# Scores ahead of values in a decode attention loop, and the last projection ahead of the first piece of w4

## The chip, the cores and the metric

The kernel runs on one core of a Trainium2 chip; the other cores are idle. The metric is device microseconds of one execution. Every run quoted here was labelled "fast" (the undisturbed state). A clock of 0.50 means that the throttle granted TensorE half its clock in that stretch. A kernel's time is the median of its runs; a ratio of two kernels is the mean time of one kernel's fast runs over the mean of the other's fast runs of the same rounds, so it is not quite the ratio of the medians that are quoted. A profile's span is about 1.8 us shorter than the time of the same execution (209.6 us for 211.45 us), because it runs from the first to the last instruction.

## The reference, cut to what matters

Two branches read the same layer-normalised input and are added: a decode step of attention with a long K/V window, and an MLP mixer with one token.

```python
# x: (4, 1, 576).  A_k_cache, A_v_cache: (4, 16, 8192, 128) bf16, the last W = 2048 keys are used
xn = layernorm(x)
# A: 32 query heads, 16 K/V heads, head size 128
q = xn @ wq
p = softmax(q @ k[:, :, -W:].T * Dh**-0.5)
attn = (p @ v[:, :, -W:]) @ wo                  # wo: 4096 x 576
# B (one token, so the shifted groups are all zero and x1 = xn)
mlp = xn + gelu(layernorm(xn) @ w3) @ w4         # w3: 576 x 4608, w4: 4608 x 576
out = x + attn + mlp
```

All of it is done for four tokens. Arithmetic is small against the data: 16 K tiles and 16 V tiles of 2.1 MB each (2048 KB, called 2 MB below), wq 4.7 MB, wo 4.7 MB, w3 5.3 MB and w4 5.3 MB are read once, 87.17 MB in all.

## The kernel before: the parts that matter

One queue issues all large loads, in a fixed order. K and V tiles rotate through six buffers; a load waits until the buffer's last reader is done. w4 comes last, in six pieces, the last ones small, so that little work is left when the last byte arrives.

```python
NKV = 6
kvp = ctx.enter_context(tc.tile_pool(name="kv", bufs=NKV))
...
W4_PIECES = [0, NFH, NF - 12, NF - 6, NF - 2, NF - 1, NF]      # NFH = 18, NF = 36
order = [("K", 0), ("K", 1), ("K", 2)]
for h in range(Hkv):                                           # Hkv = 16
    order.append(("V", h))
    if h + 3 < Hkv:
        order.append(("K", h + 3))
```

The loop over K/V heads is a software pipeline. Step `t` turns K of head `t` (VectorE), makes its scores (TensorE), does the softmax of head `t-1`, the values of head `t-2` and the output of heads before. A step has four slices `s`. An engine takes its instructions in the order in which they stand here.

```python
for t in range(Hkv):
    hm, hv, hf, hp = t - 1, t - 2, t - 3, t - 4
    for s in range(NSL):
        ...                          # softmax of hm, o_scale(hf), K transposes on VectorE
        if hv >= 0:
            pv(hv, s)                # 4 matmuls, 32 x 512 out, reads V of head hv
        k_scores(t, s)               # 4 matmuls, 128 x 512 out, reads the transposed K of head t
        ...
    flush_loads()
```

After the loop, the softmax and the values of the last two heads are finished, `o_spread` and `o_pick` prepare the last attention output, and the output matmuls are added up in two PSUM tiles, `acc` and `acc_odd`, in pairs that run side by side in different columns of the array.

```python
o_spread(hl)                 # TensorE: R
o_pick(hl)                   # VectorE: two instructions, op <- R
mlp_out(*pieces[0])          # 36 matmuls with w4 rows 0..17
o_proj(hl)                   # 16 matmuls with the last wo tile; needs op
mlp_out(*pieces[1])          # 12
mlp_out(*pieces[2])          # 12
mlp_out(*pieces[3])          # 8
...                          # odd <- acc_odd
for lo, hi in pieces[4:]:
    mlp_out(lo, hi)          # 2 + 2, on acc alone
...                          # fin = acc + odd, store
```

## Time and profile before

| | before |
|---|---|
| time | 211.55 us, median of 3 (211.48 to 211.74) |
| profile span | 209.6 us |
| DMA: load queue, share of 16 engines' span | 97.6% |
| bytes loaded | 87.17 MB |
| TensorE busy | 145.8 us (70%) |
| VectorE busy | 113.6 us (54%) |

Lines of the page of before. The rows with digits cut the span into 40 slices, in tenths: busy share for an engine, granted clock for PEclk. The q1 line is the load queue: packets, MB, and the time of its packets as a share of 16 engines' span.

```profile
PE   0367297659691009659899898597883976979884
PEclk9999589996997556958999999799998596969999
DMA  7999999999999999999999999999999999999992
q1 hardware_dynamic: 6640, 87.17, 97.6%
```

The DMA row is full from the second slice to the last but one. TensorE, at 70%, has holes, and its granted clock falls to half now and then. The Trainium skill, "HBM Reference", section "Specifications (TRN2)", says that a core streaming alone measures about 425 GB/s. Here, counted from the first packet at 1.78 us, the stream moves 87.17 MB in 204.8 us, 426 GB/s. The stream runs at the rate that the page gives.

The issues of w4's six pieces in before (durations in ns, starts in us), with the time from issue to landing:

```profile
L141 SPq DMA_DIRECT2D w_sb<-in_B_w_dram x6: 327/376/587, 170.7 to 184.5; - x6
...
DMA to landing us min/median/max: 22.0/30.3/32.6
```

The last piece, issued at 184.5, landed 22.0 us later, at 206.5. What follows it is short and fixed. The chain of waits of before (start, length, what) blames TensorE's output matmuls for the end:

```profile
205.51 0.12 PE acc L183
...
205.88 0.28 PE acc L183
```

But the timeline of before (start, length, engine, line, instruction) has a step of 0.29 us between 205.59 and 205.88, where all other pairs follow each other after 0.12 us:

```profile
205.46 0.29 PE L183 MATMUL acc<-w_sb,gT 128*8 128x288 bf16 x1
...
205.59 0.29 PE L183 MATMUL acc<-w_sb,gT 128*8 128x288 bf16 x1
...
205.88 0.28 PE L183 MATMUL acc<-w_sb,gT 128*8 128x288 bf16 x1
...
207.08 0.43 DVE L617 TENSOR_TENSOR fin<-acc,odd 8x288 bf16<-8x288 f32 x1
207.55 0.36 SPq L618 DMA_DIRECT2D out_dram<-fin  x1
```

The matmul at 205.88 is the first of w4's fourth piece, which landed at 205.84. TensorE has caught up with the loads by then, and the loads set the end.

Two of before's waits (us in total, times, longest) say what TensorE waits for in the loop: V tiles, not K. In these names vn is a V tile and kn a K tile as loaded, kt a K tile turned, S scores and O values.

```profile
PE O L394 <- DMA vn<-in_A_v_cache_dram: 36.2, 10, 15.4
PE S L342 <- DVE kt L226: 4.8, 3, 4.2
```

### The profile page before, as it was taken

To read this page: it belongs to the slowest core of one execution; us is meant where nothing else is said; L and a number is where in the kernel's file an instruction comes from. 1 tells how busy PE (TensorE), PEld (TensorE's weight loads), DVE (VectorE), ACT (ScalarE), POOL (GpSimd) and SP (SyncE) were. 2 spreads that over 40 slices of the span, in tenths; PEclk is the share of its full clock that TensorE was granted. 3 is DMA by queue.
4 is the path that set the end of the run, shared out by engine and by line. 5 is a ranking of instruction groups with operands and counts; after the bars stand their busy time and mean duration, and the time that the engine had idled before them with its cause. 6 is when DMAs were issued, how large, how long until landed. Compare 5 with 4: busy or idle time off the path is not lost.

```text
span 209.6 us, 2332 instructions
## 1 busy us (share of the span) xinstructions
PE 145.8 (70%) x941; PEld 62.6 (30%) x955; DVE 113.6 (54%) x165; ACT 34.4 (16%) x66; POOL 8.9 (4%) x33
## 2 busy tenths in 40 slices
PE   0367297659691009659899898597883976979884
PEld 0122132223240003214364233143431321425363
DVE  4501877892840082834903898658579174671420
ACT  7702201010220000202102222020211020202310
POOL 5600000000000000000000300000000000000000
PEclk9999589996997556958999999799998596969999
DMA  7999999999999999999999999999999999999992
GB/s 301 400 428 422 444 422 419 435 438 420 471 401 421 437 425 422 441 438 425 435 425 431 431 417 436 435 435 427 422 447 422 417 440 441 419 435 449 410 402 76
DMA packets 6658, 87.31 MB, mean 417 GB/s; under 512 B 748, under 2 KB 1016, under 8 KB 1656
## 3 DMA queue, kind: packets, MB, share of 16 engines
q1 hardware_dynamic: 6640, 87.17, 97.6%
q8 instruction: 7, 0.11, 0.2%
q14 instruction: 3, 0.02, 0.0%
q10 hardware_dynamic: 8, 0.00, 0.0%
HBM read 87.17 MB, written 0.00 MB: 416 GB/s over the span
## 4 chain that ended last, share of the span: by engine, by line
DMA 60%; PE 26%; DVE 9%; ACT 2%; issue 1%; SPq 0%; DVEq 0%; ACTq 0%
DMA vn<-in_A_v_cache_dram 38%; DMA w_sb<-in_B_w_dram 16%; PE S L342 9%; DMA wq_sb<-in_A_wq_dram 6%; PE acc L183 5%; DVE kt L226 5%; PE O L394 3%; PE g_ps L460 2%; PE q_ps L286 2%; PE oT L407 2%; DVE mx L348 1%; DVE PT L376 1%; PE S L364 1%; DVE qz L318 1%; PE gT_ps L472 1%
## 5 line engine op out<-in xcount | busy, mean ns | idle before, releaser
L342 PE MATMUL S<-kt,qz 128*128 128x512 bf16 x242 | 75.4, 435 | 7.2 <-DVE kt L226 4.8
L226 DVE STREAM_TRANSPOSE kt<-kn 128x2048 int32<-128x2048 int32 x32 | 73.0, 2285 | 13.5 <-DMA kn<-in_A_k_cache_dram 12.1
L394 PE MATMUL O<-vn,PT 128*32 128x512 bf16 x256 | 27.2, 425 | 38.8 <-DMA vn<-in_A_v_cache_dram 36.2
L342 PEld LDWEIGHTS <-qz 128*128 128x128 bf16 x256 | 21.9, 104 | 44.2 <-issue 28.1
L370 ACT ACTIVATE E<-S 128x512 bf16<-128x512 f32 x16 | 9.5, 597 | 120.9 <-PE S L364 120.9
L394 PEld LDWEIGHTS <-PT 128*32 128x32 bf16 x256 | 7.3, 95 | 48.2 <-issue 41.0
L376 DVE STREAM_TRANSPOSE PT<-E 128x512 bf16<-128x512 bf16 x16 | 11.4, 710 | 15.9 <-ACT E L370 15.9
L417 DVE TENSOR_REDUCE on<-oT 128x8 bf16<-128x128 f32 x16 | 4.6, 289 | 22.0 <-PE oT L407 22.0
L401 ACT ACTIVATE O_sb<-O,rd 128x512 f32<-128x512 f32 x16 | 11.0, 686 | 15.7 <-PE O L394 15.7
L348 DVE TENSOR_REDUCE mx<-S 128x1 f32<-128x512 f32 x16 | 10.5, 658 | 1.4 <-PE S L342 1.4
L407 PE MATMUL oT<-ident_w,O_sb 128*128 128x128 f32 x64 | 10.8, 295 | 0.4 <-ACT O_sb L401 0.3
L407 PEld LDWEIGHTS oT<-ident_w,O_sb 128*128 128x128 f32 x64 | 8.7, 155 | 5.5 <-issue 2.7
L360 DVE TENSOR_REDUCE nm<-mg 8x1 bf16<-8x16 f32 x16 | 2.3, 141 | 11.4 <-PE mg L355 11.4
L364 PE MATMUL S<-nm,j_row 8*128 8x512 bf16 x16 | 6.1, 381 | 2.4 <-DVE nm L360 2.3
L183 PE MATMUL acc<-wo_sb,op 128*8 128x288 bf16 x56 | 7.5, 286 | 0.0
L380 PEld LDWEIGHTS dn<-rs,same_j 128*128 128x128 f32 x32 | 5.8, 189 | 2.9 <-ACT E L370 0.7
L330 PE MATMUL S<-negbig,ohT 4*128 4x512 bf16 x16 | 6.2, 385 | 0.2 <-issue 0.2
L286 PE MATMUL q_ps<-wq_sb,xnT 128*32 128x512 bf16 x40 | 4.2, 596 | 1.8 <-DMA wq_sb<-in_A_wq_dram 1.8
L183 PEld LDWEIGHTS <-op 128*8 128x8 bf16 x64 | 4.7, 87 | 2.2 <-issue 0.3
L183 PE MATMUL acc<-w_sb,gT 128*8 128x288 bf16 x38 | 5.1, 286 | 0.0
L478 DVE COPY g_x<-gT_ps 128x64 f32<-128x64 f32 (+1 forms) x3 | 0.6, 194 | 8.4 <-PE gT_ps L472 8.4
L460 PE MATMUL g_ps<-w_sb,ln2T 128*32 128x512 bf16 (+1 forms) x50 | 4.9, 445 | 0.0
(93 smaller groups left out, 81.9 us busy)
## 6 DMA issues: line engine op xcount, KB each, us to landing
kn<-in_A_k_cache_dram SPq DMA_DIRECT2D x16, 2048.0 KB, 22.8
vn<-in_A_v_cache_dram SPq DMA_DIRECT2D x16, 2048.0 KB, 24.8
wo_sb<-in_A_wo_dram SPq DMA_DIRECT2D x4, 1152.0 KB, 25.4
w_sb<-in_B_w_dram SPq DMA_DIRECT2D x1, 4608.0 KB, 33.4
wq_sb<-in_A_wq_dram SPq DMA_DIRECT2D x1, 4096.0 KB, 12.7
w_sb<-in_B_w_dram SPq DMA_DIRECT2D x1, 2592.0 KB, 29.6
w_sb<-in_B_w_dram SPq DMA_DIRECT2D x2, 864.0 KB, 31.8
w_sb<-in_B_w_dram SPq DMA_DIRECT2D x2, 576.0 KB, 32.6
```

The costliest lines, as they stand in the source:

```text
L183: nc.tensor.matmul(out=to[q:q + OR, :], lhsT=lhsT[:, NI - 1 - i:NI - 1 - i + OR], rhs=rhs[:, i * CW:(i + 1) * CW], start=start, stop=False ...
L226: nc.vector.transpose(out=kt[:], in_=src)
L286: nc.tensor.matmul(out=q_ps[r][g * QD:(g + 1) * QD, :], lhsT=xnT[:, k, :], rhs=wq_sb[:, col:col + NW], start=(j == 0), stop=False, skip_gr ...
L342: nc.tensor.matmul(out=S_ps[h][:], lhsT=qz[:, z0:z0 + P], rhs=kt[:, ib, c0:c0 + SC, e:2 * QD:2].rearrange("p c k -> p (c k)"), start=False ...
L348: nc.vector.reduce_max(out=mx[:], in_=S_ps[h][:], axis=AX.X)
L364: nc.tensor.matmul(out=S_ps[h][:], lhsT=j_row[:], rhs=st.pop(("nm", h))[:, 0:1].to_broadcast([NJ, NW]), start=False, stop=False, skip_grou ...
L370: nc.scalar.activation(out=E[h][:].rearrange("p c k -> p (c k)"), in_=S_ps.pop(h)[:], func=ACT.Exp, scale=scale, accum_out=rs[:])
L376: nc.vector.transpose(out=PT[h][:], in_=E.pop(h)[:])
L394: nc.tensor.matmul(out=O_ps[h][g * QD:(g + 1) * QD], lhsT=PT[h][:, c, :], rhs=vn[:, :, c, :], start=(s == 0), stop=False, skip_group_check ...
L401: nc.scalar.activation(out=O_sb[h][:], in_=O_ps.pop(h)[:], func=ACT.Copy, scale=st.pop(("rd", h))[:, 0:1])
L407: nc.tensor.transpose(out=oT[:, s, :], in_=o[:, s, :], identity=ident_w[:, s * NJ:s * NJ + P])
L460: nc.tensor.matmul(out=g_ps[g * QD:(g + 1) * QD], lhsT=ln2T[:, k, :], rhs=rhs, start=(j == 0), stop=False, skip_group_check=True)
```

## The change

The intent: values need V of head `t-2`, whose load comes after that of K of head `t`. With the values first in each slice, TensorE can stand in front of a V tile with scores ready behind it. The change puts the scores of a slice first and does the values one slice later, the last two slices of values together. At the end, the last output projection, 16 matmuls whose weights came long ago, goes ahead of w4's first piece.

```diff
-            if hv >= 0:
-                pv(hv, s)
             k_scores(t, s)
+            if hv >= 0 and s > 0:
+                pv(hv, s - 1)
+                if s == NSL - 1:
+                    pv(hv, s)
...
     o_spread(hl)
     o_pick(hl)
+    o_proj(hl)
     mlp_out(*pieces[0])
-    o_proj(hl)
     mlp_out(*pieces[1])
```

No instruction is added or removed; only TensorE's order changes.

## The prediction

> **What bounds the kernel now.** The DMA stream. The page has the core's 16 DMA engines busy at 9 tenths or more in every one of the 40 slices but the first and the last, and the one big load queue takes 97.6% of 16 engines' span. It moves 87.17 MB; landing times of the loads (issue time plus time to landing, by tile) show 2 MB tiles landing every 4.85 us without a gap, and the last piece of w4, issued at 184.5, landing 22.0 us later, at 206.5. The Trainium skill, "DMA: Bandwidth & Descriptors", section "Measured", has 425 GB/s for one core's 16 MB load; here it is 87.17 MB over 204.8 us, 426 GB/s: no room is left in the stream. What follows the last landing is fixed: the last two output matmuls, VectorE's fin (207.08 to 207.52), the store's issue at 207.55, span end 209.6.
>
> The chain of waits puts the last 5 us down to "PE acc" (201.1 to 206.7), as if TensorE's output matmuls bound the end. The timeline says no: these start in pairs every 0.12 us, but between 205.59 and 205.88 there is a step of 0.29 us: a 0.17 us pause for the fourth piece of w4. TensorE has caught up with the DMA before the end.
>
> **What the change does.** No work is added or removed; TensorE's order alone changes.
> 1. In each loop step the scores of a slice no longer stand behind values that may not have landed. TensorE waits 36.2 us in total for V tiles (waits view); it can now do two slices of scores (8 matmuls, 2 to 3.8 us by clock) first. At the last step it stood until 184.53 for V13, though the transposed K was ready near 183.4. I estimate scores 15 done near 192 instead of 194.4, by removing this 1.1 us and by having one value slice (0.4 us) or more fewer ahead of each score slice.
> 2. V buffers are freed by the last values of a step, which now come after the last scores: 1.1 to 1.9 us later relative to these, partly made up by item 1. Loads wait from 17 to 41 us between issue and landing (by tile), against 4.85 us of own transfer, so at least some 12 us of queued work shield the stream. I expect no gap.
> 3. At the end, o_proj waits for o_pick. Before, VectorE's two o_pick instructions (201.16 to 202.04) hid behind the first piece of w4 (2.2 us of matmuls). Now TensorE idles some 0.95 us there, then runs o_proj (16 matmuls, 0.97 us), then the first piece. By itself that would make TensorE's end about 0.8 us later; item 1's lead of 2 us or so (less where V15, landing near 194.3, now gates) pays for it. The pieces behind it still land at about 202.3, 204.4, 205.8 and 206.5, and the last ones set the end.
>
> **On the critical path:** nearly nothing, at most 0.1 us gained; at worst, if item 1's lead isn't there, 0.8 us lost.
>
> **Predicted:** 211.5 us, range 211.1 to 211.9. Faster by over 2%: 0.01; within 2%: 0.98; slower by over 2%: 0.01.
>
> **What would show it.** Right: w4's last landing within 0.3 us of 206.5; TensorE's wait for V tiles much smaller; an idle of about 1 us before o_proj; scores 15 done 2 us earlier; a clear wait for DMA before the second to fourth piece of w4. Wrong: a hole in the DMA row, a last landing that moved, or output matmuls back to back up to fin.
>
> **What would make it wrong:** the queue running dry because V buffers free late; a lower granted clock around 190 to 200, putting o_proj's delay on the end; a different DMA rate.

## The result, and the profile after

| | before | after |
|---|---|---|
| time, median of 6 | 211.56 us (211.47 to 211.74) | 211.57 us (211.44 to 211.75) |
| ratio | | 1.000 (0.9987 to 1.0013) |
| profile span | 209.6 us | 209.9 us |
| first load lands | 3.97 us | 4.25 us |
| last load lands | 206.55 us | 206.81 us |
| between the two | 202.58 us | 202.55 us |
| scores of head 15 end | 194.41 us | 190.60 us |

Same time. The 0.3 us by which the profiled execution of after is longer is there when the first load lands, and stays.

The page of after, the lines that answer to those above. The DMA row is as full as before.

```profile
PE   0378198699670039649998999659995976898684
PEclk9999769999996557976999999999997968899969
DMA  8999999999999999999999999999999999999991
q1 hardware_dynamic: 6640, 87.17, 97.5%
```

w4's issues in after, and their time to landing:

```profile
L141 SPq DMA_DIRECT2D w_sb<-in_B_w_dram x6: 327/328/587, 168.5 to 184.6; - x6
...
DMA to landing us min/median/max: 22.2/31.7/34.6
```

w4's first piece was issued 2.3 us earlier than before (168.46 for 170.75), and only waited longer in the queue. The waits of after, of TensorE and of VectorE's K transposes:

```profile
PE S L342 <- DVE kt L226: 31.3, 13, 15.0
DVE kt L226 <- DMA kn<-in_A_k_cache_dram: 25.0, 8, 14.6
PE O L394 <- DMA vn<-in_A_v_cache_dram: 8.4, 8, 3.0
```

The wait for V fell from 36.2 to 8.4 us, and the wait for transposed K rose from 4.8 to 31.3 us; behind that one stands VectorE's own wait for K loads (12.1 us before). The idle time was moved from one kind of load to the other: these two waits of TensorE add up to 41.0 us before and 39.7 us after.

The end of after in the timeline (idle time before an instruction and what ended it are in brackets):

```profile
194.51 1.05 PE L394 MATMUL O<-vn,PT 128*32 128x512 bf16 x16 [0.62 <-DMA vn<-in_A_v_cache_dram]
...
198.76 0.29 PE L183 MATMUL acc<-wo_sb,op 128*8 128x288 bf16 x1 [0.97 <-DVE op L439]
...
200.70 0.40 PE L183 MATMUL acc<-w_sb,gT 128*8 128x288 bf16 x1 [0.78 <-DMA w_sb<-in_B_w_dram]
...
200.89 0.44 PE L183 MATMUL acc<-w_sb,gT 128*8 128x288 bf16 x1
201.13 0.44 PE L183 MATMUL acc<-w_sb,gT 128*8 128x288 bf16 x1
...
205.84 0.29 PE L183 MATMUL acc<-w_sb,gT 128*8 128x288 bf16 x1
...
206.12 0.28 PE L183 MATMUL acc<-w_sb,gT 128*8 128x288 bf16 x1
```

TensorE reaches the end 3.3 us earlier than before (the values of head 15 start at 194.51, before at 197.84). Then it waits for the last V tile, for `o_pick`, and for w4's first piece, which lands only at 200.65. After these waits the pairs of output matmuls follow each other after 0.24 us and not 0.12 us, until about 204. At 205.84 to 206.12 there is again a small pause for the fourth piece: it just fits.

Why 0.24 us? The windows view gives, for the stretch just before and the stretch itself, busy time and count of each engine, the granted clock (PEclk), the DMA share and GB/s. First before, then after:

```profile
198.00:200.70 2.70, 2.13 (x24) 1.12 (x17) 0.57 (x2) 0.81 (x2) 0.00 (x0) 1.00 0.94 397
200.70:204.00 3.30, 3.23 (x58) 2.42 (x59) 0.86 (x3) 0.00 (x0) 0.00 (x0) 1.00 0.99 405
```

```profile
198.00:200.70 2.70, 1.15 (x18) 0.73 (x18) 0.67 (x2) 0.00 (x0) 0.00 (x0) 0.98 0.89 370
200.70:204.00 3.30, 3.30 (x28) 1.90 (x29) 0.00 (x0) 0.00 (x0) 0.00 (x0) 0.50 1.00 419
```

In after TensorE was busy only 1.15 of the 2.70 us before w4's first piece, and then had half its clock for 3.4 us: 28 matmuls in a stretch in which before did 58. So the equal times needed an explanation after all. Was the loop's gain eaten by the end, or was nothing there to gain?

### The profile page after: what moved, and what is told of

The parts are those of the page before. It is cut to its first block, busy times and chain, and to the rows that moved or that the text cites. A ratio compares the mean times of both kernels' runs of the same rounds, so it can differ in the third digit from the quotient of the medians.

```text
span 209.9 us, 2326 instructions
## 1 busy us (share of the span) xinstructions
PE 149.1 (71%) x941; PEld 60.2 (29%) x955; DVE 113.7 (54%) x165; ACT 34.4 (16%) x66; POOL 8.9 (4%) x33
## 4 chain that ended last, share of the span: by engine, by line
DMA 52%; PE 24%; DVE 19%; issue 2%; ACT 1%; SPq 0%; DVEq 0%; ACTq 0%
DMA vn<-in_A_v_cache_dram 19%; DMA w_sb<-in_B_w_dram 15%; DVE kt L226 14%; DMA kn<-in_A_k_cache_dram 12%; PE S L342 9%; DMA wq_sb<-in_A_wq_dram 6%; PE acc L183 4%; PE O L394 2%; PE g_ps L460 2%; PE q_ps L286 2%; DVE mx L348 2%; PE S L364 1%; PE oT L407 1%; DVE PT L376 1%; DVE dm L350 1%
## 5 line engine op out<-in xcount | busy, mean ns | idle before, releaser
L342 PE MATMUL S<-kt,qz 128*128 128x512 bf16 x242 | 74.0, 429 | 34.5 <-DVE kt L226 31.3
L342 PEld LDWEIGHTS <-qz 128*128 128x128 bf16 x256 | 24.0, 108 | 63.5 <-issue 46.6
L394 PE MATMUL O<-vn,PT 128*32 128x512 bf16 x256 | 22.9, 400 | 8.4 <-DMA vn<-in_A_v_cache_dram 8.4
L394 PEld LDWEIGHTS <-PT 128*32 128x32 bf16 x256 | 5.9, 94 | 29.6 <-issue 28.6
L407 PEld LDWEIGHTS oT<-ident_w,O_sb 128*128 128x128 f32 x64 | 7.0, 146 | 4.6 <-issue 3.9
L183 PE MATMUL acc<-w_sb,gT 128*8 128x288 bf16 x38 | 6.6, 342 | 0.8 <-DMA w_sb<-in_B_w_dram 0.8
L380 PE MATMUL dn<-rs,same_j 128*128 128x1 f32 x32 | 6.4, 268 | 0.0
L380 PEld LDWEIGHTS dn<-rs,same_j 128*128 128x128 f32 x32 | 5.2, 204 | 4.1 <-issue 3.4
L183 PE MATMUL acc_odd<-w_sb,gT 128*8 128x288 bf16 x34 | 6.1, 350 | 0.0
```

Of the source, the lines that this page charges most:

```text
L183: nc.tensor.matmul(out=to[q:q + OR, :], lhsT=lhsT[:, NI - 1 - i:NI - 1 - i + OR], rhs=rhs[:, i * CW:(i + 1) * CW], start=start, stop=False ...
L342: nc.tensor.matmul(out=S_ps[h][:], lhsT=qz[:, z0:z0 + P], rhs=kt[:, ib, c0:c0 + SC, e:2 * QD:2].rearrange("p c k -> p (c k)"), start=False ...
L380: nc.tensor.matmul(out=dn[:], lhsT=same_j[:], rhs=st.pop(("rs", h))[:], start=True, stop=True)
L394: nc.tensor.matmul(out=O_ps[h][g * QD:(g + 1) * QD], lhsT=PT[h][:, c, :], rhs=vn[:, :, c, :], start=(s == 0), stop=False, skip_group_check ...
L407: nc.tensor.transpose(out=oT[:, s, :], in_=o[:, s, :], identity=ident_w[:, s * NJ:s * NJ + P])
```

## The experiments

Theory A, that of the prediction: the stream of loads sets the end, and TensorE's order is hidden behind it. Rival B: the loop's part gains time, and the swap at the end takes it back. Each kernel was timed beside runs of before on the same chip.

### One half of the change at a time

`loop_only` has the first hunk of the diff, `end_only` the second.

> The loop's new order without the swap at the end. Theory A (the load stream sets the end, TensorE's order is hidden behind it): same as before within 0.15 us, the last landing of w4 2.0 us or more after TensorE could have taken it, a wait of 2 us or more for w4's first piece. Theory B (the loop's part gains, the swap at the end takes it back): 0.5 to 1.5 us faster than before, about 210.5.

> The swap at the end without the loop's new order. Both theories: TensorE idles 0.95 us before o_proj and nothing pays for it; before had only a 0.17 us pause there, so the end should come 0.8 us later, 212.3 us, if the granted clock stays full; the last landing of w4 does not move. A third theory C (all that TensorE does at the end is hidden): 211.55.

| kernel | median us | lowest to highest | ratio to before |
|---|---|---|---|
| before (11 runs) | 211.63 | 211.43 to 212.00 | |
| loop_only (6) | 212.96 | 212.39 to 213.43 | 1.0064 (1.0049 to 1.0079) |
| end_only (6) | 212.02 | 211.49 to 214.11 | 1.0034 (1.0002 to 1.0067) |

Both were misses. The loop's half alone is slower, by 1.3 us, where A had the same time and B a gain. The swap is not what takes a gain back; it is what keeps the loop's half from costing. The stream hardly moved: in `loop_only` the last load landed at 207.02, 202.88 us after the first, which is 0.3 us more than in before. Most of the time is lost after TensorE's wait for w4's first piece. Timeline of `loop_only`:

```profile
197.67 0.35 PE L426 MATMUL R<-on,sel_wo 128*128 128x32 bf16 x8 [0.38 <-DVE on L417]
200.91 0.28 PE L183 MATMUL acc<-w_sb,gT 128*8 128x288 bf16 x1 [2.89 <-DMA w_sb<-in_B_w_dram]
...
201.40 0.45 PE L183 MATMUL acc<-w_sb,gT 128*8 128x288 bf16 x1
...
201.64 0.45 PE L183 MATMUL acc<-w_sb,gT 128*8 128x288 bf16 x1
```

and its windows, the same stretches:

```profile
198.00:200.70 2.70, 0.02 (x1) 0.03 (x1) 0.85 (x2) 0.00 (x0) 0.00 (x0) 1.00 0.90 372
200.70:204.00 3.30, 3.09 (x28) 1.93 (x29) 0.00 (x0) 0.00 (x0) 0.00 (x0) 0.56 1.01 424
```

TensorE came 3 us early, stood 2.89 us, and then had all 88 output matmuls in front of it with half its clock for 3.4 us: 14 pairs at 0.24 us, 14 x 0.12 = 1.7 us lost. With o_proj behind w4's first piece, the last matmul ended at 208.37, against 207.03 in before. Of these 1.34 us, 0.47 are the later last landing of this one execution, and 0.87 are work that was left after it (1.35 us from the last landing to the end of the matmuls, 0.48 in before). In after the 16 matmuls of o_proj ran inside the wait, so only 72 were left, and these just made it.

`end_only` has three runs at the time of before (211.49 to 211.62) and three above it (212.43, 212.74, 214.11). Its profile is of one of the slower ones (212.43), and shows a clock of 0.50 from 200.7 to 204.0 after the 0.97 us idle before o_proj:

```profile
198.00:200.70 2.70, 1.15 (x16) 0.84 (x18) 1.41 (x4) 0.14 (x1) 0.00 (x0) 1.00 0.94 395
200.70:204.00 3.30, 3.30 (x30) 1.82 (x28) 0.00 (x0) 0.00 (x0) 0.00 (x0) 0.50 0.99 410
```

The other five runs have no trace, so why three of them took no longer than before is not shown. Theory E: what loses time is the halved clock, falling on the output matmuls. Its rival F: the order of `loop_only` is too long for the time left after 200.9 at any clock.

### Keeping TensorE busy, or taking the wait away

`loop_fill` and `end_fill` are those kernels with filler matmuls into a scratch PSUM tile that nobody reads (12 and 4 of them); `after_fill` has 4 fillers before o_proj and 4 after it.

```diff
+    def keep_warm(n):
+        w = ps_m.tile([P, NW], F32, tag="m", name="warm")
+        for _ in range(n):
+            nc.tensor.matmul(out=w[:], lhsT=ident_bf[:], rhs=qz[:, 0:NW], start=True, stop=True)
...
     o_pick(hl)
+    keep_warm(12)                 # loop_fill
     mlp_out(*pieces[0])
```

`loop_split` removes the wait in another way: w4's first piece is loaded as three.

```diff
-    W4_PIECES = [0, NFH, NF - 12, NF - 6, NF - 2, NF - 1, NF]
+    W4_PIECES = [0, 6, 12, NFH, NF - 12, NF - 6, NF - 2, NF - 1, NF]
...
-    mlp_out(*pieces[0])
+    for i in range(3):
+        mlp_out(*pieces[i])
     o_proj(hl)
...
```

> loop_only with 12 matmuls of 512 columns into a scratch PSUM tile, read by nobody, put where TensorE idled 2.9 us before w4's first piece. Theory E (loop_only lost its 1.4 us because the granted clock was 0.5 for 3.41 us right after that idle, so that 14 pairs of output matmuls took 0.24 us each and not 0.12): no halved clock after 200, pairs at 0.12 us, 211.5 to 211.7. Rival F (the order first piece, then o_proj, is too long for the time left after 200.9 at any clock): 88 matmuls of 0.06 us are 5.4 us, so the end stays at about 213, or later by the filler's overrun.

> loop_only with w4's first piece of 18 rows loaded as three of 6, so that TensorE can begin on the first third at about 198. It takes away the wait, not the clock. Theories E and F both: 211.4 to 211.8, since 1.5 us of matmuls move ahead of 200.9. If it stays above 212.4, both are wrong and the loop's order costs something elsewhere.

> end_only with 4 such filler matmuls where TensorE idled 0.97 us before o_proj. end_only ran from 211.5 to 214.1. Theory E: that spread is the halved clock falling on the output matmuls or not; with the filler it narrows to 211.5 to 211.8. Rival: the spread has another cause and stays, over 1 us from lowest to highest.

> The changed kernel with 4 filler matmuls before o_proj and 4 between o_proj and w4's first piece. The changed kernel's profile has the halved clock from 200.6 to 204.0, yet it ended with the stream. Theory A: with a full clock TensorE waits clearly for w4's second, third and fourth piece, and the time is the same as before within 0.15 us. Rival G (the halved clock ate a gain that the change would have had): 210.5 to 211.

| kernel | median us | lowest to highest | ratio to before |
|---|---|---|---|
| before (11 runs) | 211.63 | 211.44 to 212.14 | |
| loop_fill (5) | 211.52 | 211.48 to 211.61 | 0.9991 (0.9978 to 1.0004) |
| loop_split (5) | 211.78 | 211.73 to 211.88 | 1.0003 (0.9991 to 1.0015) |
| end_fill (6) | 211.69 | 211.50 to 212.55 | 1.0007 (0.9990 to 1.0024) |
| after_fill (5) | 211.53 | 211.44 to 211.71 | 0.9992 (0.9980 to 1.0004) |

Twelve useless matmuls make `loop_only` 1.4 us faster (the two were timed on different chips, but before took 211.63 us in the median on both). Its windows and timeline with the filler:

```profile
198.00:200.70 2.70, 2.41 (x15) 1.05 (x14) 0.46 (x2) 0.00 (x0) 0.00 (x0) 1.00 0.91 375
200.70:204.00 3.30, 3.30 (x58) 2.56 (x54) 0.00 (x0) 0.00 (x0) 0.00 (x0) 1.00 1.01 421
```

```profile
197.42 2.75 PE L492 MATMUL warm<-qz,ident_bf 128*128 128x512 bf16 x12
200.47 0.28 PE L183 MATMUL acc<-w_sb,gT 128*8 128x288 bf16 x1 [0.29 <-DMA w_sb<-in_B_w_dram]
...
205.90 0.28 PE L183 MATMUL acc<-w_sb,gT 128*8 128x288 bf16 x1 [0.49 <-DMA w_sb<-in_B_w_dram]
```

The clock stays full, 58 matmuls fit into the stretch again, and TensorE waits 0.49 us for the fourth piece. E holds, and F falls: at a full clock, the order of `loop_only` is done in time. `loop_split` agrees: without the long wait the loop's half costs nothing either, and its profile has the full clock from 178.4 us to 209.

`after_fill` answers the question left by the profile of after. With a full clock from 178.6 to 209.3 us (its profile) it is no faster: rival G, that the halved clock ate a gain, falls. TensorE then starts w4's third and fourth piece late for no other reason than the loads: steps of 1.14 us at 203.44 and 0.76 us at 205.19, where pairs otherwise follow after 0.12 us.

```profile
204.58 0.28 PE L183 MATMUL acc<-w_sb,gT 128*8 128x288 bf16 x1 [0.85 <-DMA w_sb<-in_B_w_dram]
...
205.95 0.28 PE L183 MATMUL acc<-w_sb,gT 128*8 128x288 bf16 x1 [0.47 <-DMA w_sb<-in_B_w_dram]
```

`end_fill` is inconclusive. Its profiled run has the full clock, as E wants, and four of its six runs lie between 211.50 and 211.77; but two lie at 212.28 and 212.55, so the spread is still 1.05 us, just over the bound set for the rival. These two runs have no trace. In before's own profile a halved clock falls on the last loop step (0.50 from 184.9 to 188.3), a place that this filler does not reach; it may be that. It stays open.

What comes before a halved stretch? In each of the fourteen traces the halved stretches last 3.41 us or a whole multiple of it, and they lie on one grid of 3.41 us, whose place differs from trace to trace. So the window to look at is the step of that grid just before (from the clock records and the windows view; before_4buf and after_no_v15 are kernels of the next sections):

| trace | grid step, us | TensorE busy in it, of 3.41 us | clock of the next step |
|---|---|---|---|
| loop_only | 197.71 to 201.12 | 0.52 | 0.50 |
| after | 197.17 to 200.58 | 1.50 | 0.50 |
| end_only | 197.29 to 200.70 | 1.80 | 0.50 |
| after_no_v15 | 197.30 to 200.71 | 2.44 | 1.00 |
| loop_fill | 198.57 to 201.98 | 3.12 | 1.00 |
| before | 181.51 to 184.92 | 1.91 | 0.50 |
| loop_split | 202.25 to 205.66 | 1.92 | 1.00 |
| before_4buf | 196.34 to 199.75 | 2.52 | 0.50 |

The first five, all at the wait for o_pick or for w4's first piece, follow the busy time: after_no_v15 idled the same 0.97 us before o_proj and kept its clock. The last three show that it is no clean threshold. That the grid lies elsewhere in each execution may be why end_only and end_fill scatter; no run here tests it.

### A shorter stream: is there a lead on TensorE at all?

`before_no_v15` and `after_no_v15` do not load the last V tile; head 15 uses V of head 14. The result is wrong (the comparison with the reference is too loose to notice one head). That takes 2 MB or 4.85 us out of the stream.

```diff
-        order.append(("V", h))
+        if h < Hkv - 1:
+            order.append(("V", h))
...
         kv_tiles[kind, h] = t
+        if (kind, h) == ("V", Hkv - 2):
+            kv_tiles["V", Hkv - 1] = t
```

> Before, with the last V tile not loaded (head 15 uses V of head 14; wrong result on purpose): 2 MB or 4.85 us fewer in the stream. Theory A: the stream ends 4.85 us earlier but TensorE's chain, which began its output matmuls at 201.05, hardly moves: 211.0 to 211.5, only 0.1 to 0.6 us faster. Theory C: 206.7.

> The changed kernel with the same 2 MB taken away. Theory A: the change's lead on TensorE, hidden so far, comes out: 208 to 209 us, 2.5 to 3.5 us faster than the kernel before with the same cut. Theory D (the change gives TensorE no lead worth the name): the same as that kernel within 0.5 us.

In the profiles w4's last piece landed at 201.93 and 201.92 us, 4.6 and 4.9 us earlier than in before and after. before_no_v15 took 210.25 us in the median (210.14 to 211.92, 6 runs), after_no_v15 208.90 (208.83 to 208.96, 4 runs). The last output matmuls of before_no_v15, then of after_no_v15, end 5.1 and 2.1 us after that:

```profile
206.37 0.65 PE L185 MATMUL acc<-w_sb,gT 128*8 128x288 bf16 x4
```

```profile
203.41 0.65 PE L185 MATMUL acc<-w_sb,gT 128*8 128x288 bf16 x4
```

So with the loads out of the way TensorE's chain is the end in both, and the change is worth 1.35 us by the medians (1.6 us by the means, 210.51 and 208.90). Both misjudged in size: I had expected 2.5 to 3.5 us from the profile of before, and before_no_v15 at 211.0 or more. Its profiled run is the slowest of its six, 211.92 us, and has the halved clock of the last loop step (0.50 from 185.1 to 188.5) that before's profile has too; the other five took 210.14 to 210.29. It is likely that this one stretch overstated TensorE's backlog by about 1.7 us (3.41 us at half the clock loses 1.7), but the five others have no trace to show that they lack it. The lead is real and hidden: theory A, with theory D (no lead) fallen. Both hunks of the change are in it; their shares were not taken apart here.

### Fewer buffers: does the new order free V later?

The prediction's second item feared that V buffers free later. With fewer K/V buffers the queue of waiting loads is shorter, and the time of freeing begins to count. The edit is `NKV = 6` to 4, and to 3.

> Before with 4 K/V buffers for 6. Loads waited at least 17 us from issue to landing; two buffers fewer take 2 x 4.85 us of that, so the estimate is 2 to 3 us of queued work left at the worst place. Theory A: 211.5 to 213. If the stream runs dry: above 214.

> The changed kernel with 4 K/V buffers. Theory H (scores no longer wait behind values, so a step ends earlier and V buffers come free earlier on the clock, as issue times of the changed kernel's trace are 0.6 to 2.2 us earlier from 113 to 158 us): the same as or up to 2 us faster than before_4buf. Theory I (my prediction's item 2: freed later): 0.5 to 2 us slower than before_4buf.

> Before with 3 K/V buffers: no queue left, the stream has holes and a step's order on TensorE is on the path. 225 to 260 us, an estimate with little behind it; DMA row with holes.

> The changed kernel with 3 K/V buffers. Theory H: 5 us or more faster than before_3buf, since each of 13 steps has up to 2 us less wait on TensorE before K's buffers turn over. Theory I: slower than before_3buf, since V buffers free after the last scores.

| K/V buffers | before, us | after, us | difference of medians |
|---|---|---|---|
| 6 | 211.56 | 211.57 | 0.0 |
| 4 | 214.71 (214.44 to 216.51) | 213.09 (212.84 to 214.09) | 1.6 |
| 3 | 229.88 (228.21 to 230.59) | 225.73 (224.87 to 227.08) | 4.15 |

Theory H holds: the sooner the loads depend on the steps, the more the new order is worth, and item 2 is refuted in its direction. With three buffers I had put the gain at 5 us or more; it is 4.15 (3.8 by the means). before_4buf ran drier than expected (214.71 for at most 213): I had reckoned each buffer as 4.85 us of queued work. Rows of before_4buf, then after_4buf, GB/s in 40 slices:

```profile
GB/s 296 406 431 431 428 425 434 422 437 423 458 436 396 437 428 433 426 437 425 437 425 302 348 400 432 431 440 429 425 425 437 418 443 431 428 428 439 413 411 55
```

```profile
GB/s 299 397 422 438 432 419 435 432 424 438 489 419 377 438 429 415 445 432 429 429 432 363 425 410 441 447 408 435 444 413 435 425 441 441 410 438 437 410 411 45
```

The hole is in slices 22 to 24 (302, 348, 400) of before_4buf, around 112 to 128 us; in after_4buf one slice there has 363. It comes with the step that carries the MLP's w3 matmuls (102.5 to 112.8 us) and so takes long. Two loads came too late. In windows of 2 us the rate of before_4buf falls to 172 GB/s at 114 to 116 us and to 221 at 120 to 122; a V load was issued at 114.01 us and a K load at 119.88. The K load landed 8.7 us later, the shortest time to landing seen among the K and V loads of that run. With six buffers the loads in the same places in the order were issued at 98.83 and 104.61. Two buffers fewer mean that a load waits for a reader two releases later, and around that step two releases took 15 us and not 9.7. In after_4buf they were issued at 113.01 and 117.74.

## Why the prediction was right, and where it was wrong

The time was right: 211.5 us was predicted, 211.57 measured, and for the reason given. The stream from first to last landing took 202.58 us before and 202.55 after, and the same tail follows it. Some luck was in it: step 4 below failed, and what took its place was hidden with 0.16 us to spare in after's profile. Point by point:

1. "no room is left in the stream": shown. Six kernels with the full data and six buffers whose first and last landings I read (before, after, end_only, loop_fill, end_fill, after_fill) lie between 202.33 and 202.72 us; loop_only, at 202.88, is the one a little above.
2. Scores no longer behind values: right in direction, short in size. TensorE's wait for V fell to 8.4 us, and scores 15 ended at 190.6 us, not "near 192". Part of this is the halved clock at 184.9 to 188.3 us in before's profile, which after's does not have there. I also had not said that the wait would come back as one for K (31.3 us).
3. V buffers "1.1 to 1.9 us later relative to these, partly made up": wrong as a net effect. Loads were issued earlier: the last K load at 153.3 us for 155.2, w4's first at 168.5 for 170.7. Fewer buffers showed it as time, 1.6 and 4.15 us.
4. The end was the step that failed: "By itself that would make TensorE's end about 0.8 us later; item 1's lead of 2 us or so [...] pays for it." The runs showed nearly the reverse. The loop's half (item 1 of the prediction) alone costs 1.3 us (loop_only 212.96 us for 211.63), and the swap brings that back. I listed when the pieces behind w4's first one land, and forgot the first: it landed at 200.30 us in before, and a TensorE that comes 3 us earlier must wait for it. o_proj, whose data are there, is just what fits into this wait. The swap by itself (end_only) cost 0.4 us in the median.
5. "a clear wait for DMA before the second to fourth piece": in after's profile seen only before the first (0.78 us) and, tiny, before the fourth; with the full clock (after_fill) it is there, before the third and fourth. The halved clock stretched the work so that it filled the time. The risk "a lower granted clock around 190 to 200, putting o_proj's delay on the end" came about a little later, from 200.6 to 204.0, and was hidden with 0.16 us to spare (205.84 to 206.12, less the 0.12 us step). The probability of "same" was right, but less safely than I thought.

What is settled: the stream sets the time of before and after; the change is a real gain for TensorE, worth 1.35 us when 2 MB of loads go away; coming early without work in hand cost 1.3 us in loop_only, and filling the idle time, which kept the clock full in the profile, took that back; o_proj in that place avoids it. What is open: the exact rule by which the clock halves (the busy time in the grid step before tells these tails apart, but is no clean threshold over all traces), the two slower runs of end_fill, and how much of the 1.35 us is the loop's.

No version beat both kernels: loop_fill (211.52) and after_fill (211.53) stand at the same floor. What is left to gain lies in bytes, or in the 3 us after the last landing.

## What to carry to other kernels

A saturated load stream set the end here, so a better order on a compute engine gave nothing. In loop_only it was not harmless either: the engine came early, waited, and had to do much of its last work at half clock. List when every input of the tail lands, the first one too, and put work whose data are already there into the waits. Test a hidden gain by shortening the stream or the queue, and suspect a single profile wherever the granted clock differs from run to run.

## What the Trainium skill lacked or had wrong

- "TensorE: Matmul & The Clock Gate", section "HAM oscillation — how this bites in real kernels", gives the rule "no PE-idle gaps >~3.4µs". That is not enough here: a gap of 0.97 us in end_only, with TensorE busy 1.15 of the 2.70 us around it, was followed by a clock of 0.50 from 200.7 to 204.0 us; so was 2.89 us in loop_only. The length of the halved stretch, 3.4 us, does agree with the window of that page's section "What's actually happening". Busy time before, and not one gap's length, is what told these tails apart (halved after 1.50, 1.80 and 0.52 of 3.41 us; full after 2.44 and 3.12), from five profiles only; elsewhere 1.91 was followed by half the clock and 1.92 by the full one.
- No page that I read says that useless matmuls can pay: 12 of them took loop_only from 212.96 to 211.52 us. The page just named speaks of keeping TensorE warm by restructuring the loop or by padding.
- "DMA: Bandwidth & Descriptors", section "Where 436 GB/s comes from", says that for HBM to SBUF transfers the HBM side, about 358 GB/s, binds. One core alone had 426 GB/s here, which agrees with that page's own 425 GB/s for a 16 MB load and with "HBM Reference"; the sentence does not hold for the streams that were measured here.
